# Another token order for the first convolution and the front behind it, and another place for the product buffers of the first attention core

## The chip, the core and the metric

The kernel runs on one core of one Trainium2 chip. A core has TensorE (PE, matrix products into PSUM), VectorE (DVE), ScalarE (ACT), GpSimd (POOL) and SyncE (SP), which here issues the DMA transfers. Each engine works through its own instructions in the order in which the program gave them, and waits on semaphores for the others. The metric is the device time of one execution in microseconds (us).

## What is computed

A residual stream x of 2048 positions and 512 channels passes through four layers: attention, convolution, attention, convolution. Cut to what matters:

```python
x = x + A(layernorm(x), wqkv, wo)          # dilated local attention, 32 heads of 16
x = x + B(layernorm(x), A_re, ..., Dskip)  # long convolution per channel
x = x + A(layernorm(x), wqkv, wo)
x = x + B(layernorm(x), A_re, ..., Dskip)

# A: each position sees itself and 7 others, 2, 4, ... 14 positions back
logits = einsum("bhsd,bhswd->bhsw", q, k[idx]) * scale
o = einsum("bhsw,bhswd->bhsd", softmax(where(mask, logits, -1e9)), v[idx])

# B: a kernel K of 2048 taps for each channel, by a Fourier transform of length 4096
K = einsum("dn,dnl,dn->dl", C, exp(dt * A * l), dt * B).real
y = irfft(rfft(u) * rfft(K))[:2048] + u * Dskip
```

Both convolutions use the same K, so its spectrum is made once, in the first convolution, and kept in DRAM for the second.

## The kernel before

The program has six stages: tables for K together with the first projections (`k_gen`), the first attention core (`LayerA.core`, layer 0), the first convolution (`FftB`, tag 0, order `ORDER0`), its end interleaved with the projections of the second attention (`ORDERF`), the second attention core, and the second convolution (`ORDER1`).

**The attention core.** For each of four blocks of 512 positions and each of four feature tiles, `mult` (from L289) lets VectorE multiply queries with eight shifted copies of the keys into a buffer of 8 KB for each partition, and `lsum` (L298) sums the products over each head on TensorE. In layer 0 the first three products are made already in `k_gen` (`first_logits`), into `A_pr` and `A2_pr`, which are taken from the memory of a table set that is no longer needed. From the fourth product on `mult` takes buffers from the pool `self.prp`, two buffers named `prod` used in turn. `core` opens its pools one after the other: `big` (the values `v_ext`), `prp`, `wk` (the small tiles of the softmax), `pavp` (products of weights and values). A pool opened later lies behind the earlier ones in SBUF, over memory that earlier stages used, and the first write to a buffer waits for the last reader of what lay there. In the program as built the first `prod` buffer overlaps `A2_pr`, so its first write waits for the sum that reads `A2_pr`.

Behind the logits come a maximum (`mx`), an exponential, a normalisation and, for each of 16 row tiles, a product with the values (`pav`, L402), its sum (L410) and the output projection (L422). The value projections (L349) stand between the logit sums on TensorE; when the last of them is there, two DMAs shift the values by a row (L354, L355), for the rows that look over a tile's edge.

**The convolution** is written as a list of tokens. Each token names a step and, with a last letter A or D, the engine (ScalarE or VectorE) that moves its result from PSUM to SBUF. `run` (L840) goes through the list, and what it emits keeps that order on each engine:

| token | TensorE | evacuation | other |
|---|---|---|---|
| K, U | first step of the transform of the taps (K) or of the input (U), eight channels at a time: 16 matmuls (L744) | A or D | behind each K one entry of the list `late` |
| k | second step for the taps, 16 matmuls (L751) | A or D, into a buffer from the list `free` | `pump`, then a store to `kf_dram` (L761) |
| u | second step for the input (L751) | ScalarE, into `ub` (three buffers) | |
| m | none | none | VectorE multiplies `ub` with the spectrum and with its partner, two instructions (L791); the two spectrum buffers return to `free`; `pump` |
| y | inverse first step, 16 matmuls (L816, L817) | A or D | |
| z | inverse second step with the residual (L831 to L833) | A: copy (L838, TensorE adds the residual), D: addition (L836) | |

There are two groups of channels, with 8 tokens of each kind in each group. A y needs all eight m of its group, a z all y of its group, a k all K of its group, a u all U. TensorE writes four PSUM tiles in turn, so a token's matmuls wait for the evacuation four tiles back.

The partner of a spectrum is the same data with real and imaginary rows exchanged. It is made by two DMAs of half the rows each (`kf_load`, L777). `pump` (L767) issues them when the spectrum is there, and at most `ahead` (4) beyond the number of m done. `free` begins with 12 buffers and gains 8 when the last K is done (`open_ring`); what an m returns is used again.

`late` holds what the attention core leaves to be done under the convolution: the normalisation of the last row tiles (`u_end`, `u_apply` on GpSimd), statistics of tiles 14 and 15 (`x_stats`), the aggregate and the reciprocal root of the last four (`u_begin`), and two masks.

**The front** (`ORDERF`) holds, besides the remaining y and z, the layer norm of the second attention by blocks of four row tiles: h (half statistics), a (aggregate), p (reciprocal root on ScalarE), n (normalised copy), S (changes PSUM pools), T (16 transposes), E (evacuation of transposes), P (a key projection, four matmuls), Q (a query projection) and x (a copy for the tile's edge).

Of the kernel before, what the change touches and what calls it, by code (L numbers as in the profile page):

```python
# [14 lines left out]
F32 = mybir.dt.float32  # L15
BF16 = mybir.dt.bfloat16
# [4 lines left out]
P = 128  # L21
S = 2048
# [15 lines left out]
NG = 2  # L38
DQG = 64
EC = 16  # L40
NEC = 128 // EC
# [6 lines left out]
zktkKkUEETkeUUktKTkkUkKTUUeKkkpkxpKUxkpUEUxUKkqUxUUUUpqoUkpoxKXUQxoUkpkKXZpxXxpxZZ  # L48
"""
ORDER0 = """  # L50
KA KD KA KD KA KA KD KA KD KA KD kA KD KA KA kD kA kD kA UA KD UA UA UD UA kD UA
UA UD KA UA kD u kD m u u u kA m UA m UD UA u kA m kD u UA u m UA m
UD m UA kA u kD kD u kA u m m kA m u u yD yA m u u m u m yA u yA
yA m m yA m yA yD
"""
ORDERF = """
yA yA yA yA yA yA z00D yA h00 yA z01D h01 z10A z11A h10 a0 p0 h11
n0 z12A z02A a1 z03A h12 S T0 h02 p1 E00A n1 E01A a2 z13A P00 h13 Q00
h03 T1 E10A p2 E11D P01 a3 P02 P03 P10 p3 P11 n2 n3 P12 T2 E20D E21A
P13 T3 E30A P20 P21 x1 P22 P23 E31D  # L60
"""
ORDER1 = """
UD UA UA UD UA UA UD UA UD UA UD u UD u m UA u u m UA m u u UA m UD m
# [35 lines left out]
def row_stats(nc, lnst, x_row, a, eng):  # L99
    if eng == "dve":  # L100
        nc.vector.bn_stats(lnst["bn"][:, a, 0, :], x_row)
    else:
        nc.scalar.activation(lnst["junk"][:], x_row, ACT.Identity, accum_out=lnst["s1"][:, a:a + 1])
        row_sumsq(nc, lnst, x_row, a)
# [11 lines left out]
def rstd_act(nc, pool, var):  # L116
    rstd = pool.tile(list(var.shape), F32, name="ln_rstd")
    nc.scalar.activation(rstd[:], var, ACT.Ln, bias=EPS)
    nc.scalar.activation(rstd[:], rstd[:], ACT.Exp, scale=-0.5)
    return rstd  # L120
# [24 lines left out]
def ln_end(nc, pool, st):  # L145
    rstd, mean, ms = st
    nb = pool.tile(list(rstd.shape), F32, name="ln_nb")
    nc.vector.scalar_tensor_tensor(nb[:], mean, ms, rstd[:], ALU.mult, ALU.mult)
    return rstd, nb
# [6 lines left out]
def ln_apply(nc, out_ap, in_ap, rstd, nb, a, eng):  # L156
    if eng == "act":
        nc.scalar.activation(out_ap, in_ap, ACT.Identity, bias=nb[:, a:a + 1], scale=rstd[:, a:a + 1])  # L158
    else:
        (nc.gpsimd if eng == "pool" else nc.vector).tensor_scalar(out_ap, in_ap, rstd[:, a:a + 1], nb[:, a:a + 1], ALU.mult, ALU.add)  # L160


class LayerA:
# [143 lines left out]
    def core(self, x_sb, u, lnp, ev=None, nprod=0):  # L307

        tc, nc, lnst, l = self.tc, self.nc, self.lnst, self.layer
# [11 lines left out]

        with ExitStack() as c2:
            big = c2.enter_context(tc.tile_pool(name=f"a{l}_big", bufs=1, reuse_waits="tile"))
            self.prp = c2.enter_context(tc.tile_pool(name=f"a{l}_prod", bufs=2, reuse_waits="tile"))
            v = big.tile([P, NA + 14, D], BF16, name="v_ext")
            if self.wv is None:
                self.load_wv(big)
# [1 line left out]
            if l:  # L329
                self.load_wo(big)  # L330
            wk = c2.enter_context(tc.tile_pool(name=f"a{l}_wk", bufs=2, reuse_waits="tile"))
            pavp = c2.enter_context(tc.tile_pool(name=f"a{l}_pav", bufs=2, reuse_waits="tile"))
            ps_q = c2.enter_context(tc.tile_pool(name=f"a{l}_ps_q", bufs=2, space=PSUM))
            ps_o = c2.enter_context(tc.tile_pool(name=f"a{l}_ps_o", bufs=2, space=PSUM))
# [60 lines left out]
            pvs, oTs, lns = {}, {}, {}  # L395
# [35 lines left out]
            def x_stats(a):  # L431
                row_stats(nc, lnst, x_sb[:, a, :], a, "dve")

            def u_begin(a0, a1, eng, rs="pool"):
                lns[a0] = ln_begin(nc, lnp, lnst, a0, a1, eng, rs)

            def u_end(a0):
                lns[a0] = ln_end(nc, lnp, lns[a0])

            def u_apply(a0, rows, eng=None):  # L440
                rstd, nb = lns[a0]
                for a in rows:
                    ln_apply(nc, u[:, :, a, :], x_sb[:, a, :].rearrange("p (q r) -> p q r", r=4), rstd, nb, a - a0,
                             eng or ("dve" if a % 2 else "act"))
# [47 lines left out]
            for n in range(16):  # L492
# [11 lines left out]
                if n in (8, 12):  # L504
                    u_end(n - 8)
# [12 lines left out]
                if n == 15:  # L518
                    x_stats(13)
                    if l == 1:  # L520
                        u_end(8)
                        u_apply(8, range(8, 12), "dve")
# [4 lines left out]
                event(("o", n))  # L527
            if l == 0:
                out_proj(15)
                return [lambda: [u_end(8), u_apply(8, range(8, 12), "pool")], lambda: x_stats(14), lambda: x_stats(15),  # L530
                        lambda: u_begin(12, 16, "dve", "act"), lambda: [u_end(12), u_apply(12, range(12, 16), "pool")]]
            u_begin(12, 15, "dve", "act")
            out_proj(15)
            pw = pq_tile()
# [159 lines left out]
class FftB:  # L694
# [59 lines left out]
    def k_f2(self, g, ec, eng):  # L754
        n = g * NEC + ec
        p2 = self.f2(g, "ka", ec)
        kf = self.nat[n] = self.free.pop(0)
        self.evac(kf, p2, eng)
        self.nk += 1
        self.pump()  # L760
        self.nc.sync.dma_start(self.kf_dram[g, ec].rearrange("p r q e -> (p r) (q e)"), kf.rearrange("p q e -> p (q e)"))  # L761

    def open_ring(self):
        kp2 = self.ring_pool.tile([P, 8, DQG, EC], BF16, name="kf_nat", tag="kp")
        self.free += [kp2[:, i] for i in range(8)]

    def pump(self):  # L767
        while self.nkf < min(self.nk, self.nm + self.ahead):
            self.kf_load(self.nkf)
            self.nkf += 1  # L770

# [14 lines left out]
    def u_mult(self, g, ec):  # L786
        n = g * NEC + ec
        kn, ks = self.kf.pop(n)
        ub = self.ub.pop(n)
        for t, k in zip(self.S[g]["t"], (kn, ks)):  # L790
            self.nc.vector.tensor_tensor(t[:, :, ec * EC:(ec + 1) * EC], ub[:], k, ALU.mult)  # L791
        self.nm += 1
        if self.tag == 0:
            self.free += [kn, ks]
        self.pump()

# [464 lines left out]
def kernel(  # L1261
# [16 lines left out]
    nc = tc.nc  # L1278
# [6 lines left out]
    with tc.tile_pool(name="ctmp", bufs=1) as tmp:  # L1285
        consts = build_a_consts(tc, nc, cpool, tmp)
    lnst = dict(s1=cpool.tile([P, NA], F32, name="ln_s1"), s2=cpool.tile([P, NA], F32, name="ln_s2"),
                bn=cpool.tile([P, NA, 2, 6], F32, name="ln_bn"), junk=cpool.tile([P, D], BF16, name="ln_junk"),
                mh=cpool.tile([P, 4], F32, name="ln_mh"))
# [7 lines left out]
    u = xnT[:].rearrange("p t (b r) -> p (t b) r", r=64).rearrange("p q (a r) -> p q a r", r=4)  # L1297
    la = LayerA(tc, nc, consts, lnst, A_wqkv, A_wo, 0, xnT, 2)

    with tc.manual_schedule(engines=MAN):  # L1300
        C = k_gen(tc, nc, consts["ident"], ins, kd, la, x_v, lnst, lambda sp: build_b_consts(nc, cpool, sp, w2_dram))
    xpool = ctx.enter_context(tc.tile_pool(name="xres", bufs=1))
    lnp = ctx.enter_context(tc.tile_pool(name="ln_small", bufs=3, reuse_waits="tile"))
# [5 lines left out]
    kp = kpp.tile([P, P, NA, 4], BF16, name="k_perm", tag="kp")  # L1309
# [26 lines left out]
    with tc.tile_pool(name="ctmp_g2", bufs=1) as g2tmp, tc.manual_schedule(engines=MAN):  # L1336
# [6 lines left out]
              ("p", 6): [lambda: k_half_fix(0), K(0, 0)], ("p", 7): [K(0, 1)], ("p", 8): [lambda: la.load_w2(w2_dram), K(0, 2)], ("p", 9): [K(0, 3)],  # L1343
              ("p", 12): [lambda: k_half_fix(1), K(1, 0)], ("p", 13): [K(1, 1), K(1, 2)], ("p", 14): [K(1, 3)]}
        late = la.core(x_sb, u, lnp, ev, 3)
    late.append(C["masks"])
    krctx2.close()
    la.close_logits()

# [1 line left out]
    fb = FftB(tc, nc, C, consts["ident"], w2_dram, g2_dram, kf_dram, x_sb, 0)  # L1351
# [1 line left out]
    fb.ahead = 4  # L1353
    fb.open_mid()
    with tc.manual_schedule(engines=MAN):
        fb.run(ORDER0, u, k=kp, late=late)
    fb.c_mid.close()
    la.close()
    la = LayerA(tc, nc, consts, lnst, A_wqkv, A_wo, 1, xnT, 1)
# [1 line left out]
    with tc.manual_schedule(engines=MAN):  # L1361
# [21 lines left out]
        def last(*ops):  # L1383
            def f():
                for op, *ix in ops:
# [6 lines left out]
                     e=lambda ft: la.front_ext(3, "dve", ft))  # L1392
        fb.run(ORDERF, None, more=front)
        la.front_close()
# [11 lines left out]
    fb = FftB(tc, nc, C, consts["ident"], w2_dram, g2_dram, kf_dram, x_sb, 1)  # L1406
# [48 lines left out]
```

## Time and profile before

Seven runs took 431.46 to 433.79 us, with a median of 431.91. The execution that was profiled took 434.11 us; its span from the first to the last instruction is 432.3 us, at a mean granted TensorE clock of 0.995.

| stretch, us from the span's start | what runs | length | PE busy | DVE busy | ACT busy | PE clock |
|---|---|---|---|---|---|---|
| 0 to 107.4 | tables, first projections | 107.4 | 52.4 | 105.3 | 93.9 | 1.00 |
| 107.4 to 199.4 | first attention core | 92.0 | 87.6 | 86.3 | 62.1 | 1.00 |
| 199.4 to 222.4 | convolution up to the first m | 23.0 | 20.1 | 18.3 | 20.0 | 0.93 |
| 222.4 to 250.1 | from the first m to the last | 27.7 | 22.8 | 26.3 | 26.4 | 1.00 |
| 250.1 to 283.0 | rest of the first convolution, front | 32.9 | 32.4 | 24.3 | 27.7 | 1.00 |
| 283.0 to 378.7 | second attention core | 95.7 | 93.0 | 89.5 | 57.4 | 1.00 |
| 378.7 to 432.3 | second convolution | 53.6 | 43.0 | 42.0 | 38.4 | 0.99 |

Busy times are those of one engine; several engines work at a time, so a row's busy times add up to more than its length. An engine that is busy for nearly the whole stretch is a candidate for what bounds it; where several are nearly full, the order of their waits decides.

### The profile page before, as it was taken

Reading aid. Unit: us, or ns where it says so; the run is one execution under the profiler, and the core shown is the slowest. Engines: PE = TensorE matmul, PEld = TensorE weight load, DVE = VectorE, ACT = ScalarE, POOL = GpSimd, SP = SyncE. Lnnn points to the kernel's source line nnn. Section 1 sums busy time; section 2 is a strip of 40 time slices with the busy share of each in tenths; the row PEclk is TensorE's granted clock in tenths of the full one; section 3 lists DMA queues with packets and bytes.
Section 4 is the critical chain, followed back from the end, with each engine's and each line's share of the span. In section 5 each row is a group of like instructions: output and inputs, shape, how many; then the busy total and the mean of one; then the engine's idle time right before and its main releaser. Section 6 shows DMA issues by size and latency. Waiting matters only on the chain.

```text
span 432.3 us, 12729 instructions
## 1 busy us (share of the span) xinstructions
PE 351.2 (81%) x5502; PEld 263.2 (61%) x5502; DVE 391.9 (91%) x534; ACT 325.9 (75%) x557; POOL 39.0 (9%) x46
## 2 busy tenths in 40 slices
PE   3000259899999989998988899999999899997794
PEld 2000127667655668676877797555666777776794
DVE  8999999999899999995899859879998999889874
ACT  6999999986355488986899897855465468689961
POOL 3000300000692000002200000000000020000000
PEclk9999999999999999999899999999999999999999
DMA  7930832141116842742365770820042066215315
GB/s 216 392 97 12 86 72 70 32 78 46 29 38 185 245 129 80 264 199 101 110 222 192 264 198 6 259 79 2 14 111 49 2 265 213 82 80 175 121 33 165
DMA packets 62466, 54.16 MB, mean 125 GB/s; under 512 B 33893, under 2 KB 50890, under 8 KB 61130
## 3 DMA queue, kind: packets, MB, share of 16 engines
q1 hardware_dynamic: 62266, 53.22, 40.3%
q8 instruction: 43, 0.70, 0.7%
q10 hardware_dynamic: 144, 0.13, 0.1%
q14 instruction: 13, 0.11, 0.1%
HBM read 30.28 MB, written 13.24 MB: 101 GB/s over the span
## 4 chain that ended last, share of the span: by engine, by line
PE 50%; DVE 14%; ACT 11%; DMA 5%; issue 2%; SPq 1%; ACTq 0%; DVEq 0%
PE po L410 8%; PE pk L1150 5%; DVE prod L295 5%; PE pq L349 4%; PE pq L422 4%; PE pp L1088 4%; ACT a1s L733 4%; DVE pav L402 4%; PE L L302 3%; PE pp L242 3%; DMA v_ext<-v_ext 3%; PE pq L185 3%; PE pb L816 3%; PE pb L817 2%; DVE t L791 2%
## 5 line engine op out<-in xcount | busy, mean ns | idle before, releaser
L402 DVE TENSOR_TENSOR pav<-attn,v_ext 128x4096 bf16<-128x4096 bf16 x32 | 72.7, 2282 | 1.1 <-DMA v_ext<-v_ext 1.1
L295 DVE TENSOR_TENSOR prod<-qT,kT_ext 128x4096 bf16<-128x4096 bf16 x29 | 66.1, 2297 | 2.2 <-PE L L302 2.1
L410 PEld LDWEIGHTS <-pav 128*128 128x128 bf16 x1024 | 58.6, 98 | 13.4 <-DVE pav L402 10.0
L410 PE MATMUL po<-ident,pav 128*128 128x128 bf16 x1024 | 62.5, 219 | 5.0 <-DVE pav L402 5.0
L1078 PE MATMUL pt<-ident,x_blk 128*128 128x128 bf16 x64 | 6.3, 241 | 43.4 <-ACT x_blk L158 43.4
L990 DVE TENSOR_TENSOR A_t<-A_t,pow_t 128x1024 bf16<-128x1024 bf16 (+4 forms) x46 | 38.2, 872 | 0.2
L803 ACT CAST ub<-pb 128x1024 bf16<-128x1024 f32 x32 | 33.0, 1089 | 2.5 <-DVE t L791 2.4
L351 ACT CAST v_ext<-pq 128x512 bf16<-128x512 f32 x32 | 18.8, 586 | 21.1 <-PE pq L349 19.9
L302 PEld LDWEIGHTS <-prod 128*128 128x128 bf16 x928 | 26.8, 96 | 10.3 <-DVE prod L295 5.4
L422 PE MATMUL pq<-wop,oT 128*128 128x512 bf16 x128 | 32.8, 379 | 0.0
L1078 PEld LDWEIGHTS <-x_blk 128*128 128x128 bf16 x64 | 4.8, 108 | 45.8 <-ACT x_blk L158 44.4
L816 PE MATMUL pb<-Wp,t 128*128 128x128 bf16 x256 | 30.1, 219 | 3.0 <-ACT ub L803 2.7
L751 PE MATMUL pb<-a1s,w_sb 128*128 128x64 bf16 x768 | 27.5, 194 | 5.8 <-ACT ub L803 3.5
L1088 PE MATMUL pp<-xnT,kT_ext 128*128 128x512 bf16 x96 | 26.2, 400 | 6.1 <-ACT qT L1093 3.2
L733 ACT CAST a1s<-pb 128x1024 bf16<-128x1024 f32 x30 | 29.4, 1076 | 1.8 <-PE pb L744 1.8
L349 PE MATMUL pq<-wv,xnT 128*128 128x512 bf16 x128 | 30.7, 379 | 0.0
L751 PEld LDWEIGHTS <-w_sb 128*128 128x128 bf16 x768 | 25.1, 98 | 8.3 <-issue 7.1
L817 PE MATMUL pb<-WpJ,t 128*128 128x128 bf16 x256 | 30.1, 219 | 0.0
L413 ACT CAST oT<-po 128x512 bf16<-128x512 f32 x32 | 18.5, 579 | 15.2 <-PE po L410 15.1
L302 PE MATMUL L<-ind,prod 128*128 128x8 bf16 x928 | 27.5, 166 | 1.8 <-DVE prod L295 1.5
L733 DVE CAST a1s<-pb 128x1024 bf16<-128x1024 f32 x18 | 21.7, 1221 | 7.5 <-PE pb L744 7.3
L817 PEld LDWEIGHTS <-t 128*128 128x128 bf16 x256 | 24.9, 97 | 3.7 <-issue 2.7
(226 smaller groups left out, 855.0 us busy)
## 6 DMA issues: line engine op xcount, KB each, us to landing
w_sb<-w_dram SPq DMA_DIRECT2D x8, 1024.0 KB, 7.9
w_dram<-w_zero SPq DMA_DIRECT2D x1, 4096.0 KB, 15.2
kf_ring<-kf_dram SPq DMA_DIRECT2D x13, 256.0 KB, 3.6
kf_ring<-kf_dram SPq DMA_DIRECT2D x26, 128.0 KB, 3.6
v_ext<-v_ext SPq DMA_DIRECT2D x4, 784.0 KB, 6.6
x_blk<-in_A_x_dram SPq DMA_DIRECT2D x4, 512.0 KB, 4.2
kT_ext<-in_A_wqkv_dram SPq DMA_DIRECT2D x4, 512.0 KB, 9.4
x_sb<-in_A_x_dram SPq DMA_DIRECT2D x4, 512.0 KB, 5.1
```

Source lines behind the costliest of these rows:

```text
L295: nc.vector.tensor_tensor(pr, self.qT[q][:, ft].unsqueeze(1).to_broadcast([P, W, 4, P]), kap, ALU.mult)
L302: self.nc.tensor.matmul(L[:, al, w, ft * 8:(ft + 1) * 8], lhsT=pr[:, w, al, :], rhs=self.c["ind8"][:], start=(ft == 0 and w == 0 and al % ...
L349: nc.tensor.matmul(pp[:], lhsT=xnT[:, dt, a * P:(a + 1) * P], rhs=wv[:, dt, :], start=(dt == 0), stop=(dt == NDT - 1))
L402: nc.vector.tensor_tensor(pv[:], attn[:, n % 4].unsqueeze(2).to_broadcast([P, W, DH, H]), vap, ALU.mult)
L410: nc.tensor.matmul(po[:, ft, :], lhsT=pvf[:, w, ft * P:(ft + 1) * P], rhs=ident[:], start=(w == 0 and ft == 0), stop=(w == W - 1), skip_gr ...
L422: nc.tensor.matmul(pw[:], lhsT=oT[:, ftp, :], rhs=self.wo[:, ftp, :], start=False, stop=(ftp == NDT - 1))
L733: (self.nc.scalar.copy if eng == "act" else self.nc.vector.tensor_copy)(dst, src)
L751: nc.tensor.matmul(p2[:, j, :], lhsT=self.w2[:, ec * EC + j, :], rhs=a1s[:, ec * EC + j, :], start=True, stop=True)
L816: nc.tensor.matmul(p3[:, j, :], lhsT=t1[:, dql, :], rhs=wp_r, start=True, stop=False)
L817: nc.tensor.matmul(p3[:, j, :], lhsT=t2[:, dql, :], rhs=wpj_r, start=False, stop=True)
L990: return lambda: nc.vector.tensor_tensor(*args)
L1088: nc.tensor.matmul(pps[kind, b, ft][:], lhsT=la.wqk[:, dt, c:c + P], rhs=la.xnT[:, dt, b * 512:(b + 1) * 512], start=(dt == 0), stop=(dt = ...
```

## The change

The diff has four parts. The orders `ORDER0` and `ORDERF` are new lists of the same steps: in `ORDER0` five of the eight y of group 0 are gone, and `ORDERF` begins with them. Some evacuations change engine. The entries of `late` are now named, and a string gives their order; the aggregate and the reciprocal root, one entry before, are two. The store of a spectrum to `kf_dram` moves from the k token to the m token, and `pump` may load further ahead while `room()` says that enough buffers are free. In `core` the pool `prp` is opened behind `wk`, and in layer 0 a tile `gap` of 2 KB for each partition is put in front of it.

```diff
 ORDER0 = """
-KA KD KA KD KA KA KD KA KD KA KD kA KD KA KA kD kA kD kA UA KD UA UA UD UA kD UA
-UA UD KA UA kD u kD m u u u kA m UA m UD UA u kA m kD u UA u m UA m
-UD m UA kA u kD kD u kA u m m kA m u u yD yA m u u m u m yA u yA
-yA m m yA m yA yD
+KD KA KA KD KA KA KD KA KD KA KD kA kA KD kA KD UA UD UA UD UA kD UA UD UA KD kA
+kD u kD kA u UA m KD m u u UD UA UA UA m UD u m KA UD u m u kA kD m kA UA
+kD u kA m kA kD u m u kA m m u u yD yA u m yA u m m m u u m m
 """
+LATE0 = "a s t g r b m"
 ORDERF = """
-yA yA yA yA yA yA z00D yA h00 yA z01D h01 z10A z11A h10 a0 p0 h11
-n0 z12A z02A a1 z03A h12 S T0 h02 p1 E00A n1 E01A a2 z13A P00 h13 Q00
-h03 T1 E10A p2 E11D P01 a3 P02 P03 P10 p3 P11 n2 n3 P12 T2 E20D E21A
-P13 T3 E30A P20 P21 x1 P22 P23 E31D
+yA yA yA yA yA yA yD yA yA yA z01D yD yA yA z00A z10A z11A h01 h00 h10 a0 z12A
+p0 h11 z02A n0 a1 z03A h02 S T0 p1 E01D n1 E00A h12 a2 z13A P02 P01 h03 T1
+E10A Q00 E11D p2 P03 P00 n2 h13 P10 P12 a3 T2 E21D E20A p3 n3 P11 P13 P23 P21
+T3 E31D x1 E30A P20 P22
 """
...
             big = c2.enter_context(tc.tile_pool(name=f"a{l}_big", bufs=1, reuse_waits="tile"))
-            self.prp = c2.enter_context(tc.tile_pool(name=f"a{l}_prod", bufs=2, reuse_waits="tile"))
             v = big.tile([P, NA + 14, D], BF16, name="v_ext")
...
             wk = c2.enter_context(tc.tile_pool(name=f"a{l}_wk", bufs=2, reuse_waits="tile"))
+            if l == 0:
+                wk.tile([P, 1024], BF16, name="gap", bufs=1)
+            self.prp = c2.enter_context(tc.tile_pool(name=f"a{l}_prod", bufs=2, reuse_waits="tile"))
             pavp = c2.enter_context(tc.tile_pool(name=f"a{l}_pav", bufs=2, reuse_waits="tile"))
...
+            def u_aggr(a0, a1):
+                ag = lnp.tile([P, a1 - a0, 2], F32, name="ln_ag")
+                for a in range(a0, a1):
+                    nc.vector.bn_aggr(ag[:, a - a0, :], lnst["bn"][:, a, 0, :])
+                lns[a0] = ag
+
+            def u_rstd(a0):
+                ag = lns[a0]
+                lns[a0] = rstd_act(nc, lnp, ag[:, :, 1]), ag[:, :, 0], -1.0
...
-                return [lambda: [u_end(8), u_apply(8, range(8, 12), "pool")], lambda: x_stats(14), lambda: x_stats(15),
-                        lambda: u_begin(12, 16, "dve", "act"), lambda: [u_end(12), u_apply(12, range(12, 16), "pool")]]
+                return {"a": lambda: [u_end(8), u_apply(8, range(8, 12), "pool")], "s": lambda: x_stats(14), "t": lambda: x_stats(15),
+                        "g": lambda: u_aggr(12, 16), "r": lambda: u_rstd(12),
+                        "b": lambda: [u_end(12), u_apply(12, range(12, 16), "pool")]}
...
         self.nk += 1
         self.pump()
-        self.nc.sync.dma_start(self.kf_dram[g, ec].rearrange("p r q e -> (p r) (q e)"), kf.rearrange("p q e -> p (q e)"))
...
+    def room(self):
+        return self.tag == 0 and len(self.free) > NG * NEC - self.nk
+
     def pump(self):
-        while self.nkf < min(self.nk, self.nm + self.ahead):
+        while self.nkf < self.nk and (self.nkf < self.nm + self.ahead or self.room()):
             self.kf_load(self.nkf)
             self.nkf += 1
...
         self.nm += 1
         if self.tag == 0:
+            self.nc.sync.dma_start(self.kf_dram[g, ec].rearrange("p r q e -> (p r) (q e)"), kn.rearrange("p q e -> p (q e)"))
             self.free += [kn, ks]
         self.pump()
...
-    late.append(C["masks"])
+    late["m"] = C["masks"]
...
     with tc.manual_schedule(engines=MAN):
-        fb.run(ORDER0, u, k=kp, late=late)
+        late["."] = lambda: None
+        fb.run(ORDER0, u, k=kp, late=[late[c] for c in LATE0.split()])
```

Counted from the lists: before, `ORDER0` gives ScalarE 9 K, 12 U, 8 k, 16 u and 6 y and VectorE 7 K, 4 U, 8 k and 2 y; after the change ScalarE has 7 K, 10 U, 10 k, 16 u and 2 y and VectorE 9 K, 6 U, 6 k and 1 y. `ORDERF` has 8 y on ScalarE before, and 11 on ScalarE and 2 on VectorE after; of its eight z, 2 are on VectorE before and 1 after. Instructions of the stages before the first convolution and behind the front stay in the same order on every engine.

## The prediction

> **What bounds the kernel now.** One core, so I began with the busy shares: VectorE 91%, TensorE 81%, ScalarE 75%. No engine bounds the whole span, so I cut it at the edges of the change and read two stretches: the first attention core (107 to 199 us) and the first convolution with the front behind it (199 to 283 us).
>
> In the first core the engine timelines carry it, VectorE first, then TensorE (columns: start, duration, engine, line, operation, tiles, count, idle time before and what ended it).
>
> ```profile
> 112.11 0.43 DVE L255 COPY kT_ext<-kT_ext 128x508 bf16<-128x508 bf16 x1
> 114.62 4.49 DVE L295 TENSOR_TENSOR prod<-qT,kT_ext 128x4096 bf16<-128x4096 bf16 x2 [2.08 <-PE L L302]
> 119.03 1.22 DVE L363 TENSOR_REDUCE mx<-L 128x128 bf16<-128x1024 f32 x1
> ```
> ```profile
> 114.44 1.89 PE L349 MATMUL pq<-wv,xnT 128*128 128x512 bf16 x8
> 116.97 0.96 PE L302 MATMUL L<-ind,prod 128*128 128x8 bf16 x32 [0.64 <-DVE prod L295]
> 117.86 0.52 PE L285 MATMUL L<-maskrow,rows 1*128 1x448 bf16 x2
> ```
> VectorE stands 2.08 us before the fourth logit product (the first into a `prod` buffer), until TensorE has summed the third. From 114.6 to 195 us it is then almost never idle: this hole is paid in full.
>
> In the convolution I read stretches first (length, busy time with count for PE, PEld, DVE, ACT, POOL, then granted clock, DMA share, GB/s), then timelines.
>
> ```profile
> 202.50:206.00 3.50, 1.62 (x52) 1.34 (x48) 2.99 (x8) 1.96 (x5) 3.31 (x6) 1.00 0.03 7
> 206.00:209.40 3.40, 3.40 (x64) 3.14 (x63) 2.61 (x3) 2.40 (x3) 2.24 (x3) 0.50 0.00 0
> ```
> ```profile
> 204.49 0.21 ACT L118 ACTIVATE ln_rstd<-ln_ag 128x4 f32<-128x4 f32 x1 [1.50 <-DVE ln_ag L128]
> ```
> ```profile
> 200.56 1.22 DVE L733 CAST a1s<-pb 128x1024 bf16<-128x1024 f32 x1 [3.65 <-PE pb L744]
> ...
> 222.36 1.88 DVE L791 TENSOR_TENSOR t<-ub,w_sb 128x1024 bf16<-128x1024 bf16 x3
> ...
> 244.59 2.50 DVE L791 TENSOR_TENSOR t<-ub,kn 128x1024 bf16<-128x1024 bf16 x4 [1.40 <-DMA kn<-w_sb]
> ...
> 249.42 0.68 DVE L791 TENSOR_TENSOR t<-ub,kf_nat 128x1024 bf16<-128x1024 bf16 x1
> ```
> The last spectral product (token m15) ends at about 250.1 us, and only then can the inverse step of group 1 (y8) begin. From there to the end of the order (about 283.0) TensorE is busy 32.43 of 32.90 us. So two things set the time: when m15 ends, and the TensorE work behind it. VectorE leads to m15: its first evacuation at 200.56, m0 at 222.36, dense from there but for 1.40 us.
>
> **Prices of the tokens**, from rows of this trace. Evacuation on VectorE 1.14 us (starts 211.12 and 212.26), on ScalarE 0.92 (eight in 7.33 in the chain of waits); one m 1.21 (two multiplications, starts 0.604 apart); on TensorE K, U 0.44, k, u 0.50 (80 matmuls, five tokens, in 2.51), y 0.88 (16 starts, 0.055 apart), z on ScalarE 1.32, on VectorE 0.88.
>
> **Part 1, placement.** In the built program the first `prod` buffer no longer waits for the third sum but for the last table matmuls (L1150), which end at 111.1; the second likewise. VectorE can start at 112.54 instead of 114.62. Not all of it stays: TensorE is fed by it. Its sum of the fourth product then starts at 116.33 instead of 116.97 (0.64 of idle goes), the mask follows, and mx, which waits for the mask, moves from 119.03 to about 117.75: 1.28 us. Behind it TensorE loses waits of 0.46 and 0.20 as well, so the last value projection, its shift DMA and VectorE all come about 1.2 earlier. Bounds: 0.64 (what TensorE gives at once) and 2.08. The gap tile and the moved `wk`, `pav` buffers add waits for the table stores (L1172), issued by 127.3; first `pav` runs at 141.1: nothing, with some 10 us of cover.
>
> A rule speaks against it. The row: GpSimd works until 132.4 on index tables, and the product at 129.14 took 2.70 us instead of 2.28, the sum at 124.57 0.83 instead of 0.41 at 137.30. The Trainium skill, SBUF — State Buffer (Who interferes with whom), says that VectorE with two SBUF inputs and a GpSimd operation that reads SBUF exclude each other, the later one fully blocked. By the rule, up to one GpSimd instruction (0.7 us, from 1.38 for two at 112.39) per product that moves under GpSimd's work; by the rows about 0.4. One operation more comes under it, and mostly GpSimd waits (5.47 for two at 114.78). I take 0.1 off: **1.1 us**.
>
> **Part 2, the order.** VectorE evacuates 14 tiles before m0 in both orders (15.96 us), plus about 1.8 of statistics. It used to get the second tile, now the first: it starts at 200.11, where ScalarE starts now, instead of 200.56. After m0 start 16 m (19.36) and evacuations: 6 before (6.84, sum 26.20; measured 27.66 with the 1.40 wait, so the prices hold), 8 now (9.12, sum 28.48). Hence m15 ends at 200.11 + 17.76 + 28.48 = 246.35 plus all waits, against 250.1: 3.7 us less the waits. ScalarE is no bound: its tokens to u15 come to 41.1 us from 200.5.
>
> Waits now, in front of m0: 21.80 − 17.76 = 4.0 us. What goes: ScalarE's 1.50 behind the aggregate, since statistics, aggregate and reciprocal root each move to a later token (`g`, then `r` one K on); TensorE's gap of 1.17 at 205.88, which came from it. Laying the first 34 tokens along the three engines, each tile four behind in PSUM, leaves VectorE 0.2 idle before m0, as TensorE's slot is free each time. Whether the half clock of 206 to 209.4 goes too is unknown. The row: it came after 3.5 us in which TensorE worked 1.62, without one gap above 1.2. The Trainium skill, TensorE: Matmul & The Clock Gate (What's actually happening), asks for an idle window of about 3.4 us before the clock halves. By the rule my shorter gaps have nothing to do with it and the dip may come again, costing 3.4 x 0.5 = 1.7 us of TensorE work, some 1.3 for VectorE after its slack; by the row, about 2.5 of 3.5 us busy now, it goes. Bounds of all waits to m15: 0.2 and today's 5.4 (4.0 + 1.4). I take 1.3, near the walk. Gain 2.4.
>
> **Part 3, loads and stores.** The store of a spectrum moves behind its use; `room()` lets loads start when buffers allow, not at most four ahead. Counts stay: 16 stores, 32 half loads. The 1.40 wait at 244.59 came from loads queued behind three stores on SP at 238.3; now loads 10 to 15 are issued with their k, ahead of those stores. New: load 4 writes a buffer of m0, so it waits for m0 and for store 0. Behind it on SP stand store 1 and loads 5 to 7, and m4 to m7 wait for these. Issue 2 x 0.6 us, landing 3.5: about 5.5 us after m0 starts, needed after 9.4. The k8, k9, k14, k15 evacuations wait for stores of m2 to m5, which land before. Cost nothing while VectorE covers the 4 us.
>
> **Part 4, the front.** Five y of group 0 now follow u15, on TensorE while VectorE makes the last m: hidden. From y8 on, one z goes from VectorE to ScalarE: TensorE +0.44. Two y and one more transpose copy go to VectorE. T0 waits for n0: laid out, 0.6 us of idle; today the stretch has 32.9 for 31.6 of work, so 1.3 idle. Net 0, bounds −0.6 and +0.7. Core 1 and the second convolution keep their order and shift whole.
>
> **Sum.** 1.1 + 2.4 = 3.5 us. The profiled execution took 434.11 (span 432.3), so 430.6 there; its median sibling 431.91 gives **428.4**.
>
> **Rivals.**
> - *Likeliest, 0.63*: as above. Own range: 431.91 − 2.08 − 3.7 = 426.1 to 431.91 − 0.64 − 1.0 = 430.3.
> - *The placement is hidden anyway, 0.11*: the value shift DMA (6.05 us in the chain of waits) ends just before its `pav`. If it doesn't move, only part 2 counts: 429.5. Against: its last input moves with TensorE.
> - *The waits only change place, 0.12*: VectorE waits 5.4 us as now, on PSUM slots. Then part 2 gives 3.7 − 5.4 = −1.7, with part 1 −0.6 in all: 432.5, about no change. For it: three engines with almost equal sums to m0 (TensorE 15.4, ScalarE 17.4, VectorE 17.8).
> - *SP's queue becomes the bound, 0.14, slower*: from m0 on it carries 16 stores and 24 half loads, 40 transfers, and each waits for the one eight before it. With m15's load at least 2.6 us early, 28.5 − 2.6 = 25.9 us are there; 40 x L / 8 exceeds that from a landing L of 5.2 us, the longest seen for a ring read or store of this tensor. At 6.5: 32.5 − 25.9 = 6.6 late, 431.91 − 3.5 + 6.6 = 435.0. Against: medians of 2.0 to 3.6 now, at a DMA share of 0.6.
>
> **Numbers.** About 0.3% (1.3 us) can be told from no change. Faster: 0.63 + 0.11 + a little of the third, 0.76; same 0.10; slower 0.14. The range runs from 426.0 to 431.6; the slower case and part of the third stay outside.
>
> **To be seen in the profile after**: the first `prod` right behind the L255 copy; mx near 117.8; no 1.50 before ln_rstd and no clock of 0.50 behind it; m0 some 3 us earlier relative to the first K; no wait for a load in the m's; group 1's y dense on TensorE. Wrong it is if m0 to m15 takes over 30 us, or if the half clock returns and VectorE waits for TensorE.

## The result, and the profile after

Twelve runs of the changed kernel gave a median of 428.74 us (428.10 to 430.76), 31 of the kernel before 432.78 (431.11 to 434.30). The ratio is 0.9916, with a 95% interval of 0.9900 to 0.9933: 3.6 us faster, between 2.9 and 4.3 (the two medians lie 4.0 apart). A second comparison, further down, gave 0.9929 (0.9902 to 0.9955). The forecast was 428.4, a gain of 3.5 from a median of 431.91 over seven runs of before.

The profiled execution took 428.18 us (span 426.4). That is 5.9 us below the profiled one of before, more than the medians say, so the first question is which of the 5.9 us belong to the change. By stretches of VectorE's timeline:

| from, to | before | after | difference |
|---|---|---|---|
| start to the first evacuation of the convolution | 200.56 | 199.44 | -1.12 |
| first evacuation to first m | 21.80 | 17.70 | -4.10 |
| first m to the end of the last | 27.74 | 28.39 | +0.65 |
| end of the last m to the first product of core 1 | 34.84 | 34.53 | -0.31 |
| from there to the end | 147.36 | 146.34 | -1.02 |

The last row is not the change's: no instruction of that stage moved, and the changed kernel profiled once more (g4, below) took 148.00 us for it. Two things vary there. In nine of the fourteen profiles of this study TensorE's granted clock was halved once, 50 to 52 us into the stage, and those nine took 147.3 to 148.0 us; four of the other five took 146.3 to 146.8. The fifth is before: no half clock there, but a `pav` stood 1.12 us for the value shift's DMA at 328.86, a wait of at most 0.55 us elsewhere. So 4.9 us are left to explain, and one more piece of them will turn out to be chance.

The first core, VectorE's timeline after (columns as in the prediction):

```profile
112.07 0.44 DVE L255 COPY kT_ext<-kT_ext 128x508 bf16<-128x508 bf16 x1
112.61 4.80 DVE L295 TENSOR_TENSOR prod<-qT,kT_ext 128x4096 bf16<-128x4096 bf16 x2
117.57 1.23 DVE L365 TENSOR_REDUCE mx<-L 128x128 bf16<-128x1024 f32 x1 [0.16 <-PE L L285]
...
135.85 0.82 DVE L381 TENSOR_TENSOR s<-ex 128x512 bf16<-128x512 bf16 x1
136.71 0.67 DVE L383 TENSOR_TENSOR s<-s 128x256 bf16<-128x256 bf16 x1
```

The hole of 2.08 us is gone, and mx comes 1.46 us earlier. But the pair of products takes 4.80 instead of 4.49, and the pair of sums at the end 0.82 and 0.67. The same two before:

```profile
137.30 0.41 DVE L379 TENSOR_TENSOR s<-ex 128x512 bf16<-128x512 bf16 x1
137.74 0.29 DVE L381 TENSOR_TENSOR s<-s 128x256 bf16<-128x256 bf16 x1
```

GpSimd's timeline suggests why, and f1 and f3 below test it. First before, then after:

```profile
112.39 1.38 POOL L684 TENSOR_SCALAR g_i<-g_i,aux 128x512 int32<-128x512 int32 x2
...
126.98 5.42 POOL L684 TENSOR_SCALAR k_perm<-k_perm,aux 128x512 int32<-128x512 int32 x2
```
```profile
112.36 5.53 POOL L697 TENSOR_SCALAR g_i<-g_i,aux 128x512 int32<-128x512 int32 x2
...
131.97 5.27 POOL L697 TENSOR_SCALAR k_perm<-k_perm,aux 128x512 int32<-128x512 int32 x2
```

In VectorE's hole GpSimd scaled two index tables in 1.38 us; without the hole the same two take 5.53. Its last table ends at 137.2 instead of 132.4, so VectorE meets one more pair of sums under it.

The convolution after, in stretches of the same times as before, then ScalarE's reciprocal root and VectorE's corner points:

```profile
202.50:206.00 3.50, 3.22 (x92) 2.76 (x91) 3.50 (x9) 3.47 (x7) 2.81 (x4) 1.00 0.00 0
206.00:209.40 3.40, 3.40 (x110) 3.11 (x108) 3.24 (x4) 3.40 (x4) 1.65 (x3) 1.00 0.18 60
```
```profile
203.51 0.24 ACT L118 ACTIVATE ln_rstd<-ln_ag 128x4 f32<-128x4 f32 x1
```
```profile
199.44 1.23 DVE L746 CAST a1s<-pb 128x1024 bf16<-128x1024 f32 x1 [3.21 <-PE pb L757]
...
217.14 1.28 DVE L806 TENSOR_TENSOR t<-ub,w_sb 128x1024 bf16<-128x1024 bf16 x2
...
244.85 0.68 DVE L806 TENSOR_TENSOR t<-ub,w_sb 128x1024 bf16<-128x1024 bf16 x1
```

TensorE is busy 3.22 us of 3.50 where it was busy 1.62, the granted clock is 1.00 where it was 0.50, ScalarE has no wait before `ln_rstd`, and no m waits for a load.

### The profile page after: what moved, and what is told of

Its sections match the earlier page's. It is cut to its first block, busy times and chain, and to the rows that moved or that the text cites. A ratio compares the mean times of both kernels' runs of the same rounds, so it can differ in the third digit from the quotient of the medians.

```text
span 426.4 us, 12741 instructions
## 1 busy us (share of the span) xinstructions
PE 351.7 (82%) x5506; PEld 263.9 (62%) x5506; DVE 394.5 (93%) x537; ACT 323.7 (76%) x554; POOL 44.0 (10%) x46
## 4 chain that ended last, share of the span: by engine, by line
PE 51%; DVE 19%; ACT 7%; issue 3%; DMA 3%; SPq 1%; ACTq 0%; DVEq 0%
PE po L412 9%; PE pk L1166 5%; DVE pav L404 5%; DVE prod L295 5%; PE pq L424 4%; PE pq L351 4%; PE pp L1104 4%; PE pp L242 3%; PE L L302 3%; PE pq L185 3%; PE pb L833 3%; PE pb L832 3%; ACT ub L819 2%; DVE a1s L746 2%; DVE t L806 2%
## 5 line engine op out<-in xcount | busy, mean ns | idle before, releaser
L832 PE MATMUL pb<-Wp,t 128*128 128x128 bf16 x256 | 31.5, 225 | 1.2 <-ACT ub L819 0.7
L833 PE MATMUL pb<-WpJ,t 128*128 128x128 bf16 x256 | 31.3, 225 | 0.4 <-DVE t L806 0.4
L746 DVE CAST a1s<-pb 128x1024 bf16<-128x1024 f32 x22 | 26.1, 1217 | 4.9 <-PE pb L757 4.8
L746 ACT CAST a1s<-pb 128x1024 bf16<-128x1024 f32 x26 | 25.6, 1041 | 2.0 <-PE pb L757 2.0
L833 PEld LDWEIGHTS <-t 128*128 128x128 bf16 x256 | 25.8, 101 | 2.0 <-DVE t L806 1.2
```

The costliest lines, as they stand in the source:

```text
L746: (self.nc.scalar.copy if eng == "act" else self.nc.vector.tensor_copy)(dst, src)
L832: nc.tensor.matmul(p3[:, j, :], lhsT=t1[:, dql, :], rhs=wp_r, start=True, stop=False)
L833: nc.tensor.matmul(p3[:, j, :], lhsT=t2[:, dql, :], rhs=wpj_r, start=False, stop=True)
```

## The experiments

All ratios are to the kernel before, run beside each kernel on the same chip. The lengths are from one profile each, on VectorE: from the start of the L255 copy to the first evacuation, from there to the first m, from there to the end of the last m, and what of that the m's stood for a load. Absolute times of two profiles can be 0 to 0.4 us apart already at the copy, so only lengths are compared. (Where an expectation counts from the first K on TensorE, that lies 0.7 to 1.1 us before the first evacuation.)

| kernel | copy to first evacuation | to first m | to end of last m | load waits | ratio (interval) |
|---|---|---|---|---|---|
| before | 88.45 | 21.80 | 27.74 | 1.40 | 1 |
| changed | 87.37 | 17.70 | 28.39 | 0 | 0.9916 (0.9900 to 0.9933) |
| e1 placement alone | 87.81 | 20.29 | 27.12 | 0.77 | 0.9964 (0.9937 to 0.9991) |
| e2 orders and loads alone | 88.00 | 17.70 | 28.46 | 0 | 0.9937 (0.9907 to 0.9968) |
| e3 split alone | 88.44 | 19.62 | 27.36 | 1.01 | 0.9977 (0.9948 to 1.0006) |
| e4 changed, not split | 87.77 | 18.27 | 30.26 | 1.57 | 0.9950 (0.9920 to 0.9981) |
| f1 changed, no scaling | 85.71 | 17.69 | 28.39 | 0 | 0.9884 (0.9854 to 0.9914) |
| f2 before, no scaling | 87.56 | 20.29 | 26.28 | 0 | 0.9961 (0.9938 to 0.9985) |
| f3 scaling on ScalarE | 86.20 | 17.70 | 28.39 | 0 | 0.9891 (0.9870 to 0.9912) |
| f4 changed, no room() | 87.34 | 17.71 | 31.09 | 2.36 | 1.0006 (0.9983 to 1.0029) |
| g1 changed, old loads | 87.58 | 17.70 | 31.91 | 3.16 | 1.0005 (0.9982 to 1.0028) |
| g2 before, new loads | 88.45 | 20.29 | 26.26 | 0 | 0.9984 (0.9966 to 1.0002) |
| g3 scaling under pav | 85.64 | 17.71 | 28.39 | 0 | 0.9876 (0.9851 to 0.9901) |
| g4 changed again | 87.59 | 17.70 | 28.96 | 0.47 | 0.9929 (0.9902 to 0.9955) |

**Placement and order apart (e1, e2).** The placement alone, in the kernel before:

```diff
-            self.prp = c2.enter_context(tc.tile_pool(name=f"a{l}_prod", ...))
             v = big.tile([P, NA + 14, D], BF16, name="v_ext")
...
             wk = c2.enter_context(tc.tile_pool(name=f"a{l}_wk", ...))
+            if l == 0:
+                wk.tile([P, 1024], BF16, name="gap", bufs=1)
+            self.prp = c2.enter_context(tc.tile_pool(name=f"a{l}_prod", ...))
```

> The kernel before with part 1 alone (the gap tile, and the product buffers behind the softmax's tiles); orders, loads and stores as before. Theory A (placement given back to GpSimd): the first prod follows the L255 copy at 112.6 as in the changed kernel, mx comes about 1.4 us earlier, but GpSimd's eight tensor_scalar end near 137 instead of 132.4 and one more pair of sums (L379, L381) takes 0.8 and 0.7 us instead of 0.4 and 0.3; the first evacuation of the convolution comes only 0.5 to 0.7 us earlier and the whole is 0.6 us faster, ratio 0.9986. Theory B (the prediction's own sum): 1.1 us, ratio 0.9975. Theory C (nothing is kept, all of the gain is the order's): 0, ratio 1.000.

The same three edits taken back in the changed kernel give e2.

> The changed kernel with the product buffers back at their old place and without the gap tile: orders, late list, loads and stores as changed. Theory A (the two parts add up, the order carries most): the first part of the first attention core as before (prod at 114.6, first K at 199.4), from the first K to the first m about 18.3 us instead of 22.9, m15 some 4.0 us earlier than before; the whole 3.0 to 4.0 us faster, ratio 0.991 to 0.993. Theory B (the prediction's sum for the order): 2.4 us, ratio 0.9944. Theory C (they don't add: the order gains only what the placement lets it): below 2 us, ratio above 0.995.

In the trace of e1 the first evacuation comes 0.64 us earlier, as theory A says; the interval of its ratio holds 0.6 and 1.1 us alike but not zero, so C falls. e2 has the first m and the last m where the changed kernel has them (17.70 and 28.46), and its first evacuation 0.45 us earlier than before, because the first tile goes to VectorE. Its ratio lies between A and B, and the interval can't separate them; the traces show that the two parts add.

The surprise is in e1's other columns: it has the old order, the old late list and the old loads, and still its first m comes after 20.29 us instead of 21.80. The stretches of e1 that answer to those shown of before (its times run 0.3 us later):

```profile
202.80:206.30 3.50, 1.82 (x59) 1.68 (x60) 2.99 (x9) 2.09 (x4) 3.31 (x5) 1.00 0.00 0
206.30:209.70 3.40, 3.38 (x104) 3.02 (x99) 3.23 (x4) 3.39 (x5) 1.63 (x3) 1.00 0.08 26
...
142.20:145.70 3.50, 3.50 (x22) 2.24 (x20) 3.50 (x3) 1.17 (x2) 0.00 (x0) 0.51 0.93 241
```

The same instructions before it and the same gaps (ScalarE waits 1.50 us for the aggregate here too), yet the clock behind them is 1.00, and TensorE does 104 matmuls where it did 64. f2 and g2, further down, have that stretch unchanged as well, and both show 20.29. So the half clock cost 1.51 us in the profile of before, and of the four profiles with this stretch as it was (before, e1, f2, g2) it was the only one to pay it.

The traces show what decides. Within one profile all half clocks start whole multiples of 3.413 us apart (before: 205.97 and 431.25, 66 times; e1: 142.25, in the last line above, and 333.40, 56 times), so the clock goes by a grid of windows, and the grid lies elsewhere in each execution. On the grid of before, the window ahead of the half clock (202.56 to 205.97) held 1.53 us of TensorE work. On the grids of e1, f2 and g2 the emptiest window there held 2.2, 2.2 and 2.0 us, and no half clock followed. In the changed kernel no stretch of 3.41 us there, wherever the grid lies, holds less than 3.07 us, and no half clock in the fourteen profiles followed a window of more than 2.5. So, as far as these profiles show, the change closed the place where the clock could fall; what chance decided is that the profile of before paid the full price of it.

**The split of the late entry (e3, e4).** e3 is the kernel before with

```diff
-                        lambda: u_begin(12, 16, "dve", "act"), ...
+                        lambda: u_aggr(12, 16), lambda: u_rstd(12), ...
```

> The kernel before with one edit: aggregate and reciprocal root of the last four row tiles as two entries of the late list, one K apart; everything else as before. Theory A (the wait of ScalarE for the aggregate starts the chain of waits before the first m and with it the half clock): ln_rstd no longer waits 1.5 us, the stretch of clock 0.50 is gone, the first m comes 1.5 to 2.5 us earlier relative to the first K (22.9 before), ratio 0.994 to 0.9965. Theory B (the order of the K, U, k tokens makes the gap, the split alone only moves the wait): first m less than 0.6 us earlier, a clock of 0.50 still in one stretch before it, ratio 0.999 to 1.001.

and e4 the changed kernel with the reverse, an empty entry keeping the later ones in their place:

```diff
-LATE0 = "a s t g r b m"
+LATE0 = "a s t g . b m"
...
-                        "g": lambda: u_aggr(12, 16), "r": lambda: u_rstd(12),
+                        "g": lambda: [u_aggr(12, 16), u_rstd(12)],
```

> The changed kernel with one edit: aggregate and reciprocal root together on the K where the aggregate alone stood, an empty entry where the root stood; everything else as changed. Theory A (the split removes the waits): ScalarE waits about 1.5 us for the aggregate again, the half clock comes back, the first m is 1.5 to 2.5 us later relative to the first K than the 18.3 of the changed kernel, ratio to the kernel before 0.995 to 0.998. Theory B (the order of the tokens covers it): the first m less than 0.6 us later, no clock of 0.50, ratio 0.991 to 0.993.

Against 20.29, what the old order takes without a half clock, the split alone brings 0.67 us, and its absence costs 0.57 in the new order (18.27 against 17.70). Both theories missed in e3: against the 21.80 of before its first m comes 2.2 us earlier, as A says, but 1.51 of that is the half clock, and without it the gain is too small for A; the half clock of B isn't there. ScalarE's wait behind the aggregate was 0.59 us in e3 and 0.65 in e4, so a part of the wait of 1.50 goes with the split and a part with the order. In e3 the emptiest 3.41 us there holds 2.25 us of TensorE work, in e4 2.17. Of the 2.59 us between 20.29 and 17.70 the split makes some 0.6 and the order of the tokens 2.0. e4's first m fits its theory B and its ratio A: it loses more than 0.57 us, and in its profile m15 stood 1.57 us for its load.

**GpSimd's part (f1, f2).** Both leave out the eight `tensor_scalar` that scale the index tables; without them the tables of the inverse transform have no meaning.

```diff
             nc.gpsimd.iota(g.rearrange("p (a m) -> p a m", m=P), ...)
-            nc.gpsimd.tensor_scalar(g, g, p21, bias, ALU.mult, ALU.add)
```

> The changed kernel without the eight tensor_scalar of GpSimd that scale the index tables under the first attention core (the inverse tables of the convolution are then wrong; the instructions that read them stay). Theory A (GpSimd and VectorE take turns, and this gave back half of the placement): the first two prods take 4.49 instead of 4.80 us, every pair of sums 0.41 and 0.29 instead of 0.83 and 0.67, the prod at 127.7 2.28 instead of 2.70; together 2.3 us, first evacuation of the convolution at about 197.2 instead of 199.4; ratio to the kernel before 0.985 to 0.988. Theory B (VectorE's slower instructions come from something else, as the DMAs or ScalarE): the durations stay, first evacuation within 0.3 us, ratio 0.990 to 0.993.

> The kernel before without the same eight tensor_scalar (the inverse tables are wrong, as in the run above). Theory A: only 1.2 us come back (one pair of sums 0.8, one prod 0.4), since three of the eight ran in VectorE's hole before the fourth product; first evacuation at about 199.3 instead of 200.5, ratio 0.997; so without GpSimd the placement is worth 1.8 to 2.1 us between the two kernels' first evacuations, and 0.65 with it. Theory B: first evacuation within 0.3 us, ratio 0.999 to 1.001.

VectorE's timeline of f1:

```profile
112.78 4.49 DVE L295 TENSOR_TENSOR prod<-qT,kT_ext 128x4096 bf16<-128x4096 bf16 x2
117.74 1.22 DVE L365 TENSOR_REDUCE mx<-L 128x128 bf16<-128x1024 f32 x1 [0.47 <-PE L L285]
...
134.81 0.41 DVE L381 TENSOR_TENSOR s<-ex 128x512 bf16<-128x512 bf16 x1
135.26 0.29 DVE L383 TENSOR_TENSOR s<-s 128x256 bf16<-128x256 bf16 x1
```

Every duration that theory A named fell back as it said, and B falls. The sizes are smaller than expected, since TensorE takes a part: mx now waits 0.47 us for the mask instead of 0.16. The changed kernel gains 1.66 us without GpSimd's scaling (87.37 to 85.71), the kernel before 0.89 (88.45 to 87.56). Between f2 and f1 lie 1.85 us, of which 0.45 is the first tile on VectorE. So the placement is worth 1.40 us if GpSimd keeps out of the way, and 0.64 if not: **0.76 us of it went to GpSimd's work, which the old hole had served for nothing.**

**The scaling on ScalarE (f3, g3).** ScalarE can scale the tables. f3 spreads four pairs over the product steps:

```diff
+            nc.scalar.activation(g, g, ACT.Identity, scale=p21, bias=bias)
...
+              ("m", 1, 1): [G(ga, 0)], ("m", 1, 3): [G(ga, 1)], ("m", 2, 1): [G(ga, 2)], ("m", 2, 3): [G(ga, 3)],
```

> The changed kernel with the scaling of the index tables on ScalarE (eight activations, spread over four product steps) in place of GpSimd; the result stays the reference's. Theory A: as without the scaling, if ScalarE's eight activations of about 0.58 us delay no evacuation: VectorE's durations 4.49, 0.41, 0.29; first evacuation at 197.2 to 198; ratio to the kernel before 0.985 to 0.989, about 2 us faster than the changed kernel. Theory B (ScalarE in front of TensorE's value projections takes the place): TensorE waits for its evacuations and VectorE for the sums, first evacuation at 199 or later, ratio 0.990 to 0.993.

Its first evacuation came 1.17 us sooner than the changed kernel's, between A and B. ScalarE's pairs of 1.32 us stood in front of evacuations: TensorE waited 0.30 and 0.33 us, and a `pav` 0.53 for the value shift behind them. So g3 puts the eight, singly or in pairs, behind the last value projection, under the pav products:

```diff
+              ("p", 1): [S(0, 0)], ("o", 1): [..., S(0, 1)], ("p", 2): [S(1, 0)], ("o", 2): [G(gs, 0), S(1, 1)],
+              ("o", 3): [S(2, 0), S(2, 1)], ("o", 4): [S(3, 0), S(3, 1)],
```

> The changed kernel with the scaling of the index tables on ScalarE one instruction at a time under the pav products, behind the last value projection; the result stays the reference's. Theory A (in the earlier spread ScalarE's four pairs held back TensorE by 0.3 us twice and the value shift by 0.5): none of these waits, first evacuation at 197.9 to 198.1 as without the scaling at all, about 1.6 us before that of the changed kernel; ratio to the kernel before 0.986 to 0.989. Theory B (ScalarE's work under pav holds back other evacuations): first evacuation 198.5 or later, ratio 0.989 to 0.992.

VectorE's timeline of g3, with the lengths of f1 again:

```profile
112.63 4.49 DVE L295 TENSOR_TENSOR prod<-qT,kT_ext 128x4096 bf16<-128x4096 bf16 x2
...
134.67 0.42 DVE L381 TENSOR_TENSOR s<-ex 128x512 bf16<-128x512 bf16 x1
...
197.75 1.23 DVE L749 CAST a1s<-pb 128x1024 bf16<-128x1024 f32 x1 [3.20 <-PE pb L760]
```

Theory A, but for 0.17 us that one pav still stands: the first evacuation comes 1.73 us sooner than in the changed kernel. The median of six runs was 427.02 us, beside 429.41 for six of the changed kernel and 432.16 for the kernel before, all on one chip. f3 was not run beside the changed kernel, and its interval overlaps that kernel's.

**Loads and stores (f4, g1, g2).** In f4 `room()` always returns False, and the rest stays as changed:

> The changed kernel with room() always false: partner loads start at most four ahead of the m, as before, while the stores stay behind the m. Theory A (loads ahead of the stores keep the second half of the m dense): from about m8 on loads stand behind stores on the DMA queue, one or more m wait 1 to 3 us for a load, first to last m 29 to 31 us instead of 27.7, ratio to the kernel before 0.995 to 0.999. Theory B (room() makes no difference, the loads land in time either way): no wait of an m for a DMA, ratio 0.990 to 0.993.

In g1 the changed kernel has the old loads and stores, in g2 the kernel before the new ones (cut from g2; the store's line and `room()` move with it, and g1 is the reverse):

```diff
-        while self.nkf < min(self.nk, self.nm + self.ahead):
+        while self.nkf < self.nk and (self.nkf < self.nm + self.ahead or self.room()):
```

> The changed kernel with its new orders and placement, but with loads and stores as before: the store behind the k, loads at most four ahead, no room(). Theory A (the new order needs the new loads): m's of the second group wait 1.5 to 4 us for a partner load, m15 ends at 247 to 249.5 instead of 245.5, ratio to the kernel before 0.997 to 1.001, as with room() alone taken away. Theory B (the prediction's: loads and stores cost and give nothing beyond 1.4 us of an old wait): m15 1.4 us later at most, ratio 0.992 to 0.9955.

> The kernel before with the new loads and stores alone: the store behind the m, room(); orders, late list and placement as before. Theory A (the loads matter only where the order would otherwise run into them): no wait of an m for a load, first m where it was, gain no more than the old load wait of 1.4 us: ratio 0.997 to 1.000. Theory B (the loads carry the gain by themselves): ratio 0.991 to 0.995.

VectorE's timeline of g1, the only multiplications that wait:

```profile
240.03 1.29 DVE L804 TENSOR_TENSOR t<-ub,kf_nat 128x1024 bf16<-128x1024 bf16 x2 [0.63 <-DMA kf_nat<-kf_nat]
241.92 1.29 DVE L804 TENSOR_TENSOR t<-ub,kf_nat 128x1024 bf16<-128x1024 bf16 x2 [0.60 <-DMA kf_nat<-kf_nat]
...
247.63 0.69 DVE L804 TENSOR_TENSOR t<-ub,kf_sb 128x1024 bf16<-128x1024 bf16 x1 [1.93 <-DMA kf_sb<-kf_nat]
```

Theory A in all three (f4 a little beyond its range). The new order brings the first m 2.6 us forward, and with the old loads later ones wait 3.16 us (2.36 in f4); the ratio is 1.0005 and nothing of the order's gain is left. The new loads in the old order are worth little, if anything. Only together do they pay. In f4's and g1's profiles a half clock (247.5 to 254, and 250 to 253.5) also followed the wait, behind windows with 1.19 and 0.71 us of TensorE work, on the y that TensorE had been kept from, so those two lose more in their profiles than they waited.

**The changed kernel once more (g4).**

> The changed kernel once more, unaltered, beside the three above. Theory A (the stretches of half clock come by chance, the rest of the trace repeats): first evacuation at 199.4 to 199.8, first m 17.7 us behind it, m15 at 245.3 to 245.8, core 1 at 280.0 to 280.4 unless a stretch of clock 0.50 falls in between; half clock at other places than 396 and 424; ratio 0.990 to 0.993. Theory B (the half clock belongs to a place in the program): again at 396 and 424.

The half clocks came at 65.8, 332.0 and 427.6. Neither theory fits whole: the one at 396 did not return, but the last is that of 424, at the end of the program, and every one of the fourteen profiles ends with it. The one at 332 sits where eight other profiles have theirs. So the places repeat, and the grid decides which of them are met. The first m came 17.70 us behind the first evacuation again. But m15 stood for its load this time. The DMA queue and VectorE in g4:

```profile
241.76 1.11 SPq L792 DMA_DIRECT2D w_sb<-kf_sb  x2
```
```profile
245.99 0.69 DVE L806 TENSOR_TENSOR t<-ub,w_sb 128x1024 bf16<-128x1024 bf16 x1 [0.47 <-DMA w_sb<-kf_sb]
```

It landed 3.1 us after its second half was issued. In the profile shown of the changed kernel the same load was issued by 241.58 and needed at 244.85: a slack of 3.3 us for a landing of about 3.

## Why the prediction was right, step by step

**Part 1, placement: mechanism right, size too large.** The first product stands right behind the copy, and mx came at 117.57 (117.75 was forecast). 0.64 us was left at the first evacuation instead of 1.1: the lower bound. The mis-sized term is "I take 0.1 off" for GpSimd; f1 and f2 measure 0.76. The Trainium skill's rule on the shared port (SBUF — State Buffer, Who interferes with whom), weighed there at up to 0.7 us for each product that moves under GpSimd's work, was nearer than the choice, which took GpSimd to be the one that mostly waits. What the choice overlooked is that a part of GpSimd's work was done in the hole; without it that work ended 4.8 us later and met more of VectorE's instructions.

**Part 2, the order: the layout was right to 0.1 us, the allowances were not.** The work of VectorE was forecast as 17.76 us to the first m and 28.48 behind it; measured 17.70 and 28.39 in the changed kernel, with a single wait of 0.16 us at 206.94 (the layout had left 0.2). The 1.3 us of waits that the sum kept were not there (0.6 in g4, with its load). On the other side, the waits of today were put at 5.4 us from one execution. 1.51 of that was the half clock, and the load wait of 1.40 is 0 to 1.01 in the other profiles of the old order. Without the half clock the old order takes 46.6 us (f2, in which no m waits for a load; g2, with the new loads) to 48.0 (before, less 1.51) from the first evacuation to the end of the last m, the new one 46.1 (changed) to 46.7 (g4), and it starts 0.45 us sooner. That is a gain of 0.3 to 2.4 us; 2.4 was forecast. ScalarE's wait of 1.50 counted as a cause; its removal was worth 0.6.

**The half clock: the reading by the row was right in kind, but took one execution for all.** It said that the dip goes because TensorE would be busy about 2.5 of 3.5 us; the changed kernel is busy at least 3.07 of 3.41 there, and none of the nine profiles with the new order shows a half clock before the first m. The reading by the rule, that short gaps have nothing to do with it, fails: the window ahead held 1.53 us of work and no gap above 1.2. What the prediction overlooked is the grid: the old order pays only where a window falls on its gap.

**Part 3, loads and stores: no cost, as said, but not for the reason given.** "Cost nothing while VectorE covers the 4 us" treated them as an edit beside the order. They are what lets the order pay: without them it loses all. And the cover is thin: m15's load decides.

**Part 4, the front:** 0 forecast, 0.31 us gained in the profile (34.84 to 34.53 from the last m to the first product of core 1), inside its bounds. It repeats: the old order takes 34.8 to 35.0 in all five profiles, the new one 34.5 in all but f4 and g1, where the half clock fell on it.

**The rivals.** That the placement is hidden fell with e1. That the waits only change place fell with 17.70 us. SP's queue as the bound was the right thing to fear: f4 and g1 are that case, reached not by slower landings but by loads issued later, and in e4 and g4 the queue held m15 for 1.57 and 0.47 us.

**The sum.** Traced parts that repeat: 0.64 us of the placement, 0.3 to 2.4 of the order, 0.3 in the front, so 1.2 to 3.3 us, while the ratios say 3.6 (2.9 to 4.3) and 3.1 (1.9 to 4.2). A part of the rest is the half clock that the old order can meet and that the new one, by the windows above, does not. An estimate from the traces: the windows that would hold no more than 1.6 to 2.0 us of work there take up 17 to 41% of all positions of the grid, and 1.51 us at that chance is 0.3 to 0.6 us on average. What the value shift's landing in core 1 adds was not separated. So the forecast of 3.5 was met partly by errors that cancel: the placement was put 0.5 too high and the front 0.3 too low, and the order's 2.4 stands at the upper end of what the traces give.

## What to carry to other kernels

Before you price a stall as pure gain, look at what the other engines do in it: beside an idle VectorE GpSimd scaled two tables in 1.38 us instead of 5.53, and closing the hole gave half of its worth back (0.76 of 1.40 us). When an order of work is brought forward, its transfers must be brought forward with it; either edit alone showed no gain clear of the noise. And before a gain is built on a stretch of reduced clock seen in one profile, look for it in a second, and ask how little work a window there can hold at all, because where the windows lie changes from execution to execution.

## What the runs showed of the hardware

- In the fourteen profiles of this study TensorE's granted clock fell to 0.50 for 3.41 us at a time (6.83 once, in f4 from 247.3; 47.79 twice, in f1 and f4 from 11.7 on; the one at the end of the program varies). Within each profile these stretches start whole multiples of 3.413 us apart, and the grid lies elsewhere in each execution. The places repeat: every profile has one at its end, nine have one at 329 to 336, 50 to 52 us behind the first product of core 1, four at 64 to 66, three at 155 to 157, two at 141 to 142. The first m of the old order was met in one of four profiles with the stretch as it was, that of the new order in none of nine. After the first 60 us, and but for the end, the 3.41 us ahead of a half clock held 0.7 to 2.5 us of TensorE work. Little work alone did not bring it: windows of 1.5 us at 60 us were not followed by one in e1, e2, g2 and g3, so what exactly is counted stays open. The Trainium skill says that the window of about 3.4 us over which the clock's control looks is free-running (TensorE: Matmul & The Clock Gate, What's actually happening); the grid agrees with that, and a wholly idle window was not needed.
- Two GpSimd `tensor_scalar` of 128 x 512 int32 took 1.38 us beside an idle VectorE and 4.7 to 5.6 beside VectorE's products of two SBUF inputs; on VectorE each such meeting cost up to 0.42 us, twice the length of a short sum (0.41 to 0.83). ScalarE did the same pair in 1.32 us, and VectorE's products and sums beside it kept their length (4.49 and 0.41 to 0.42 us in f3 and g3).
